# Token mix of an fp32 mixer block: eight chunks of 512 output tokens and a separate stage for the last 128

## Chip, cores, metric

The kernel runs on one core of a Trainium2 chip. The metric is device time in microseconds (us) of one execution of the program; lower is better.

## What is computed

Three layers follow each other on x of shape [4, 4224, 192] (B batches, S tokens, D channels). Weights come as float64 and are unpacked on the chip.

```python
# 1. causal convolution over 7 tokens, softmaxed taps, one set of taps per head
out[b, s, h, g] = sum_k w[h, k] * x_pad[b, s + k, h, g]
# 2. token mix over all 4224 tokens, then a channel mix
theta = x @ w_theta                      # 192 x 192
zr, zi = x * cos(theta), x * sin(theta)
y = einsum('ts,bsd->btd', w_tok_r, zr) + einsum('ts,bsd->btd', w_tok_i, zi)   # two 4224 x 4224 weights
u = x + y;  x = u + relu(u @ w_ch)
# 3. low-rank token mix (rank 32) and a feed-forward layer 192 -> 768 -> 192
u = x + ((x.T @ U) @ V).T;  x = u + relu(u @ w_ch1) @ w_ch2
```

## The kernel before

**Data.** y is kept in one SBUF tile `yt` of 128 partitions by 6 by 4224: the 4 x 192 = 768 (batch, channel) columns are six blocks of 128 partitions, the tokens lie along the free axis. The source tokens are 33 blocks s of 128. For each block, two "units" (one per half of the batches) run a prep: convolution on VectorE (14 instructions), a split into a high and a low part, theta on TensorE (10 matmuls), range reduction on VectorE, sine and cosine on ScalarE, products on VectorE, and again a split. The result is `z` of block s: 128 source tokens by 4 (real high, imaginary high, real low, imaginary low) by 768.

**Token mix.** A group (g, j, r) makes one PSUM tile `acc` of 128 (batch, channel) columns by one chunk of output tokens. In `products` (line 709 is its matmul) a 128 x 128 block of z is stationary and the weights of the chunk move: for each source block and for real and imaginary weights the three products z_high w_high, z_high w_low, z_low w_high, all in fp32r. With two source blocks (kb = 2) that is 12 matmuls. `evict` (line 717 on VectorE, 719 on ScalarE for the first source block) adds the group to `yt`. PSUM gives `acc` four buffers.

**Steps.** `mix_steps` lists the steps. In the steady part a stage takes two source blocks through nine chunks (`WIDTHS`: 480, six of 464, two of 480), so nine steps g; the last two source blocks use eleven chunks of 384 (`LATE`), interleaved with the layers that follow. A step has six slots j. In each slot the group comes first, then the weight jobs of `SPLITS[j]`, then the prep functions that `plan` holds for that slot. All engines take their instructions strictly in this written order.

**Weights.** A step needs two pieces (q = 0 real, q = 1 imaginary), each up to 960 raw float64 words per partition, loaded on SP's queue into one of two `wraw` buffers. `split_w` does four parts: 0, two ScalarE instructions (lines 250 and 255); 1, sign and join on VectorE (264 and 269); 2, the high part by a ScalarE cast (652); 3, the low part by a VectorE subtraction (655), behind which the next load is issued. Both pieces of a step share one tile `wt[g]` of two buffers. For step g + 1, `SPLITS` spreads the parts over the slots of step g:

```python
SPLITS = [
    [(1, 0, 2)], [(1, 0, 3), (1, 1, 0)], [(1, 1, 1)], [(1, 1, 2)], [(1, 1, 3), (2, 0, 0)], [(2, 0, 1)],
]
```

Each entry is (steps ahead, q, part). So the low part of the second piece is made in slot 4, and slot 5 lies between it and the step that reads it.

**Around it.** `OPENING` is a hand-written order of the start: the first three steps, the first four units, their weights. `unit_slots` places the 20 stages of every later unit in slots; four units are spread over a stage, 12 slots apart. `ENTRY` and `TURN` are written orders for the last two source blocks, the channel mix, the low-rank mix and the start of the feed-forward layer, whose matmuls (lines 1158 to 1162 and 1195 to 1201) have 384 moving columns.

Of the kernel before, what the change touches and what calls it, by code (L numbers as in the profile page):

```python
# [10 lines left out]
F32 = mybir.dt.float32  # L11
F32R = mybir.dt.float32r
I32 = mybir.dt.int32
# [20 lines left out]
WIDTHS = [480] + [464] * 6 + [480] * 2  # L34
# [5 lines left out]
def mix_steps():  # L40
# [15 lines left out]
EARLY = 5  # L56
STEPS, STARTS = mix_steps()

# [30 lines left out]
WSTEP = 480  # L89

LSTEP = 448
# [3 lines left out]
SPLITS = [  # L95
    [(1, 0, 2)], [(1, 0, 3), (1, 1, 0)], [(1, 1, 1)], [(1, 1, 2)], [(1, 1, 3), (2, 0, 0)], [(2, 0, 1)],
]
PREP_AT = -4
UNIT = 12

STAGES = 20


def unit_slots():

    def steady(n0):
        return [n0 + n for n in range(STAGES)]

    n0 = SLOTS * OPENED
    units = [(2, 0, [n0 + n // 2 for n in range(TAPS)] + steady(n0 + 4)[: STAGES - TAPS])]  # L110
    units += [(2, 1, [n0 + 8 + n // 2 for n in range(TAPS)] + steady(n0 + 12)[: STAGES - TAPS])]
    n0 = SLOTS * STARTS[1]
    units += [(3 + u // 2, u % 2, steady(n0 - 8 + (21 * u) // 2)) for u in range(4)]
    for k in range(2, len(STARTS) - 1):
        n0 = SLOTS * STARTS[k] + PREP_AT
        units += [(2 * k + 1 + u // 2, u % 2, steady(n0 + UNIT * u)) for u in range(4)]
    return units

# [106 lines left out]
def mix_kernel(ctx, tc, xT, wcv, wth, wtok, wch, uu, vv, w1, w2, outT):  # L225
# [68 lines left out]
    wp = pool("wp", bufs=2, stack=left)  # L294
    wrp = pool("wraw", bufs=2, stack=raw_st)
# [5 lines left out]
    ps_th = pool("ps_th", bufs=2, space=PSUM, stack=prep_st)  # L301
# [4 lines left out]
    with tc.manual_schedule():  # L306
# [12 lines left out]
        wc_raw = taps(3300)  # L319
# [32 lines left out]

        def load_w(h):
            if h >= len(pieces):
                return
            kb, n, src = pieces[h]
            if h in (2, 3):
                t = spare(h - 2, 2336, 4 * WIDTHS[1]).bitcast(I32).rearrange("p (n w) -> p n w", w=2)
            else:
                t = wrp.tile([P, 2 * WMAX, 2], I32, name="wraw", tag="wraw")  # L360
# [1069 lines left out]
```

## Time and profile before

| | us |
|---|---|
| time, median of 3 runs | 2961.15 |
| lowest and highest run | 2960.17 and 2961.39 |
| span of the profiled execution, first to last instruction | 2958.9 |
| that execution: TensorE busy (matmuls) | 2947.7 |
| VectorE busy | 2494.5 |
| ScalarE busy | 1547.0 |
| GpSimd busy | 308.4 |

The profile is of one execution; its span leaves out what lies around the first and last instruction, 2.25 us against the median of the runs. PE is TensorE, PEld its weight loads, DVE is VectorE, ACT ScalarE, POOL GpSimd, SP the engine whose queue issues the loads. A matmul's "mean" is its own time from start to modelled end, and neighbours overlap in the pipeline: what a stream of them costs is read from a stretch's length divided by the count in it.

### The profile page before, as it was taken

The numbers are of one execution on the slowest core, as the hardware profiler recorded it, in microseconds if no ns is written. First come the engines' busy times: TensorE is split into PE (matmuls) and PEld (weight loads), VectorE is DVE, ScalarE is ACT, GpSimd is POOL, SyncE is SP. The second block draws the span as 40 slices with busy tenths as digits, with TensorE's granted clock in tenths as the row PEclk, the third lists the DMA queues.
The fourth block names the chain that finished last, engine by engine and source line by source line (L and its number), as shares of the span: only waits on it lengthen the run. The fifth ranks groups of instructions, "written<-read, shape, count | busy, mean of one in ns | idle before, by whom it ended". The sixth has DMA issues, their size and how long they took to land.

```text
span 2958.9 us, 39058 instructions
## 1 busy us (share of the span) xinstructions
PE 2947.7 (100%) x14994; PEld 2689.5 (91%) x14994; DVE 2494.5 (84%) x4132; ACT 1547.0 (52%) x2230; POOL 308.4 (10%) x263
## 2 busy tenths in 40 slices
PE   9999999999999999999999999999999999999999
PEld 8888888888888889898989898888889999999999
DVE  8899989888888988898989898989899887555555
ACT  7655545455555555554555554545456555444443
POOL 2110000010000000000000010100002111001000
PEclk9999999999999999999999999999999999999999
DMA  4443443443434434434434334344343221101110
GB/s 137 134 132 123 128 132 125 128 132 122 136 124 127 135 125 127 133 122 131 129 124 132 128 124 135 124 128 135 122 129 107 74 65 50 37 31 43 35 38 33
DMA packets 119003, 323.51 MB, mean 109 GB/s; under 512 B 6688, under 2 KB 40480, under 8 KB 118688
## 3 DMA queue, kind: packets, MB, share of 16 engines
q1 hardware_dynamic: 118416, 320.81, 33.7%
q8 instruction: 118, 1.93, 0.3%
q14 instruction: 69, 0.57, 0.1%
q10 hardware_dynamic: 400, 0.21, 0.0%
HBM read 308.01 MB, written 12.98 MB: 108 GB/s over the span
## 4 chain that ended last, share of the span: by engine, by line
PE 95%; DVE 3%; issue 0%; ACT 0%; DMA 0%; POOL 0%; DVEq 0%; POOLq 0%; ACTq 0%
PE acc L709 74%; PE ob L1196 2%; PE acc L1158 2%; PE acc L1162 2%; PE oa L1198 2%; PE ob L1195 2%; PE oa L1201 2%; PE oa L1200 2%; PE acc L1159 2%; PE acc L1160 2%; PE acc L1161 1%; PE pacc L916 1%; PE th L541 1%; PE th L542 1%; PE tr L901 1%; PE th L544 1%
## 5 line engine op out<-in xcount | busy, mean ns | idle before, releaser
L709 PE MATMUL acc<-w,z 128*128 128x464 f32 (+2 forms) x10836 | 2286.7, 371 | 1.8 <-POOL z L603 0.8
L709 PEld LDWEIGHTS acc<-w,z 128*128 128x128 f32 x10836 | 2015.6, 188 | 241.4 <-DVE yt L717 1.5
L717 DVE TENSOR_TENSOR yt<-acc,yt 128x464 f32<-128x464 f32 (+2 forms) x876 | 551.9, 636 | 211.8 <-PE acc L709 208.4
L652 ACT CAST w<-wraw 128x928 fp32r<-128x928 f32 (+3 forms) x281 | 294.6, 1049 | 625.4 <-DVE wraw L269 625.4
L264 DVE TENSOR_SCALAR wraw<-wraw 128x928 uint16<-128x928 uint16 (+3 forms) x305 | 369.5, 1212 | 12.3 <-ACT wraw L255 6.2
L250 ACT ACTIVATE wraw<-wraw,consts 128x928 int32<-128x928 uint16 (+3 forms) x305 | 349.1, 1144 | 23.9 <-DMA wraw<-in_wtok 16.7
L655 DVE TENSOR_TENSOR w<-wraw,w 128x928 fp32r<-128x928 f32 (+2 forms) x272 | 356.5, 1310 | 0.0
L269 DVE SCALAR_TENSOR_TENSOR wraw<-wraw 128x928 int32<-128x928 int32 (+3 forms) x305 | 342.0, 1121 | 9.8
L255 ACT ACTIVATE wraw<-wraw 128x928 f32<-128x928 f32 (+4 forms) x289 | 304.4, 1053 | 4.1 <-DMA wraw<-in_wtok 1.9
L603 POOL TENSOR_TENSOR z<-tz,z 128x384 fp32r<-128x384 f32 x121 | 125.2, 1034 | 1706.3 <-ACT z L600 1706.3
L478 DVE SCALAR_TENSOR_TENSOR xa<-xr,tap,xa 128x256 f32<-128x256 f32 x744 | 286.7, 428 | 0.0
L1170 DVE SCALAR_TENSOR_TENSOR hid<-acc,hid 128x384 fp32r<-128x384 f32 x264 | 146.8, 557 | 148.9 <-ACT hid L1167 148.0
L1167 ACT ACTIVATE hid<-acc 128x384 fp32r<-128x384 f32 x264 | 129.7, 492 | 250.1 <-PE acc L1162 232.8
L600 ACT CAST z<-tz 128x384 fp32r<-128x384 f32 x129 | 66.3, 514 | 289.0 <-DVE tz L589 288.9
L609 POOL TENSOR_TENSOR yt<-yt,xa 128x384 f32<-128x384 f32 x64 | 70.2, 1096 | 248.6 <-DVE xa L478 195.4
L1196 PE MATMUL ob<-hid,cl 128*128 128x384 f32 x264 | 89.2, 338 | 0.1
L1158 PE MATMUL acc<-fq,w 128*128 128x384 f32 x264 | 89.1, 338 | 0.0
L1162 PE MATMUL acc<-fq,w 128*128 128x384 f32 x264 | 89.0, 337 | 0.0
L1198 PE MATMUL oa<-hid,cl 128*128 128x384 f32 x264 | 88.7, 336 | 0.0
L1201 PE MATMUL oa<-hid,cl 128*128 128x384 f32 x264 | 88.7, 336 | 0.0
L1200 PE MATMUL oa<-hid,cl 128*128 128x384 f32 x264 | 88.7, 336 | 0.0
L1195 PE MATMUL ob<-hid,cl 128*128 128x384 f32 x264 | 88.6, 336 | 0.0
(244 smaller groups left out, 2685.9 us busy)
## 6 DMA issues: line engine op xcount, KB each, us to landing
wraw<-in_wtok SPq DMA_DIRECT2D x184, 928.0 KB, 4.7
wraw<-in_wtok SPq DMA_DIRECT2D x92, 960.0 KB, 4.8
wraw<-in_wtok SPq DMA_DIRECT2D x22, 768.0 KB, 4.4
xr<-in_xT SPq DMA_DIRECT2D x63, 201.0 KB, 2.7
outT<-ot SPq DMA_DIRECT2D x20, 576.0 KB, 3.1
vzw<-in_vv SPq DMA_DIRECT2D x10, 384.0 KB, 4.1
wraw<-in_w SPq DMA_DIRECT2D x3, 768.0 KB, 4.3
yt<-in_wtok SPq DMA_DIRECT2D x2, 928.0 KB, 8.6
```

Of the source, the lines that this page charges most:

```text
L250: nc.scalar.activation(words(raw, 0), words(raw, 1, U16), AF.Identity, scale=2.0**-13, bias=consts[:, 3:4])
L255: nc.scalar.activation(w, w, AF.Copy, scale=2.0**-112)
L264: nc.vector.tensor_scalar(out=words(raw, 1, U16), in0=words(raw, 3, U16), scalar1=0x8000, scalar2=None, op0=ALU.bitwise_and)
L269: nc.vector.scalar_tensor_tensor(out=words(raw, 1), in0=words(raw, 1), scalar=3, in1=words(raw, 0), op0=ALU.logical_shift_left, op1=ALU.bi ...
L478: nc.vector.scalar_tensor_tensor(out=xa, in0=src, scalar=w, in1=xa, op0=ALU.mult, op1=ALU.add)
L652: nc.scalar.copy(hi, src)
L655: eng.tensor_tensor(out=weight_part(g, q, 1), in0=src, in1=f(hi), op=ALU.subtract)
L709: mm(ps, a, b[:, i + r, :], start=n == 0, stop=n == last)
L717: nc.vector.tensor_tensor(out=dst, in0=ps, in1=dst, op=ALU.add)
L1158: mm(ps, w[0], q[:, b, :], start=True, stop=False)
L1162: mm(ps, w[3], q[:, 4 + b, :], start=False, stop=True)
L1196: mm(ob, c2[:, m, 2, :], h[:, 1, :], start=False, stop=last)
```

## The change

`WIDTHS` becomes eight chunks of 512. They cover 4096 tokens; the last 128 (`TAIL`) of 31 of the 33 source blocks go through a new function `tail`, once in each stage (15 times): there a 128 x 128 block of weights is stationary, z moves with 384 columns, and the sums come out with the tokens on the partitions. They are kept so in the last columns of `yt` and transposed once at the end (`tail_turn`). Each piece of weights gets a tile of its own (`wt[g, q]`), with four buffers of half the size, and a spare tile shifts their addresses. Two temporaries of the prep move: `ta` shares the buffer of `xq`, `tb` goes to PSUM, and theta's PSUM tile loses its second buffer. So sine and cosine now share one buffer and come one after the other. The weight jobs are listed by step (`split_plan`), with three more job slots in a step that has a tail; the units' slots are packed differently. In the opening, `EARLY` is 4, so its third step has one chunk instead of two. The two source blocks at the end keep their eleven chunks of 384.

```diff
-WIDTHS = [480] + [464] * 6 + [480] * 2
+WIDTHS = [512] * 8
+TAIL = sum(WIDTHS)
...
-EARLY = 5
+EARLY = 4
 STEPS, STARTS = mix_steps()
+TAILS = {STARTS[1] + EARLY - 1: (0, 3)} | {n + 3: (2 * k + 3, 2) for k, n in enumerate(STARTS[2:-1])}
...
-WSTEP = 480
-
-LSTEP = 448
+WSTEP = 512
+HALF = 4 * WSTEP
+SHIFT = 16
...
+def split_plan():
+
+    def following(g):
+        return ("t", g + 1) if g + 1 in TAILS else 2 * (g + 2)
+
+    plan = {}
+    for g in range(OPENED, STARTS[-1]):
+        a, b, c = 2 * (g + 1), 2 * (g + 1) + 1, following(g)
+        if g in TAILS:
+            t = ("t", g)
+            jobs = [[(t, 2)], [(t, 3), (a, 0)], [(a, 1)], [(a, 2)], [(a, 3), (b, 0)], [(b, 1)]]
+            jobs += [[(b, 2)], [(b, 3), (c, 0)], [(c, 1)]]
+        elif g == STARTS[-1] - 1:
+            jobs = [[(a, 0)], [(a, 1), (b, 0)], [(a, 2), (b, 1)], [(a, 3), (b, 2)], [(b, 3)], [(c, 0), (c, 1)]]
+        else:
+            jobs = [[(a, 2)], [(a, 3), (b, 0)], [(b, 1)], [(b, 2)], [(b, 3), (c, 0)], [(c, 1)]]
...
-PREP_AT = -4
+SPLITS = split_plan()
+PREP_AT = -8
 UNIT = 12
-STAGES = 20
+STEADY = list(range(20))
+QUICK = [*range(TAPS), 7, 8, 8, 9, 10, 11, 11, 11, 12, 13, 14, 15, 16]
...
-    units += [(3 + u // 2, u % 2, steady(n0 - 8 + (21 * u) // 2)) for u in range(4)]
+    units += [(3 + u // 2, u % 2, slots(n0 - 9 + 9 * u, QUICK)) for u in range(4)]
...
-    wp = pool("wp", bufs=2, stack=left)
-    wrp = pool("wraw", bufs=2, stack=raw_st)
+    wp = pool("wp", bufs=4, stack=left)
+    wp.tile([P, 32], F32, name="align", tag="align", bufs=1)
+    raws = {"pool": pool("wraw", bufs=2, stack=raw_st), "n": 2 * WMAX}
...
-    ps_th = pool("ps_th", bufs=2, space=PSUM, stack=prep_st)
+    ps_th = pool("ps_th", space=PSUM, stack=prep_st)
+    ps_x = pool("ps_x", space=PSUM, stack=prep_st)
...
-            stages += [(("sincos",),), (("rot", 0), ("z_hi", 0)), (("z_lo", 0, eng),)]
+            stages += [(("sincos", 0), ("sincos", 2)), (("rot", 0), ("z_hi", 0)), (("sincos", 1), ("z_lo", 0, eng))]
...
+        def tail_products(g, r):
+            s0, kb = TAILS[g]
+            key = "t", g
+            ps = sums[key, r] = ps_mm.tile([P, WMAX], F32, name="acc", tag="acc")[:, :COLS]
+            n, last = 0, 6 * kb - 1
+            for u in range(2 * kb):
+                z, q = zt[s0 + u // 2], u % 2
+                zh, zl = (z[:, m, r * COLS : (r + 1) * COLS] for m in (q, 2 + q))
+                high, low = (tail_part(key, m)[:, u, :] for m in range(2))
+                for a, b in ((high, zh), (high, zl), (low, zh)):
+                    mm(ps, a, b, start=n == 0, stop=n == last)
+                    n += 1
...
+        def tail(g):
+            tail_products(g, 0)
+            split_jobs(g, SLOTS)
+            tail_products(g, 1)
+            tail_evict(g, 0)
+            split_jobs(g, SLOTS + 1)
+            tail_evict(g, 1)
+            split_jobs(g, SLOTS + 2)
+            del wt["t", g]
 
         def mix(steps):
             for g in steps:
                 for j in range(SLOTS):
                     for r in range(len(STEPS[g][2])):
                         group(g, j, r)
-                    for d, q, part in SPLITS[j]:
-                        split_w(g + d, q, part)
+                    split_jobs(g, j)
+                    if g == max(TAILS) + 1 and j < 2:
+                        tail_turn(j)
                     for fn in plan.get(g * SLOTS + j, ()):
                         fn()
-                del wt[g]
+                for q in range(2):
+                    del wt[g, q]
+                if g in TAILS:
+                    tail(g)
```

## Rows read from the trace of the kernel before

**Rows 1.** The page: span, and each engine's busy time, share of span and instructions.

```profile
span 2958.9 us, 39058 instructions
PE 2947.7 (100%) x14994; PEld 2689.5 (91%) x14994; DVE 2494.5 (84%) x4132; ACT 1547.0 (52%) x2230; POOL 308.4 (10%) x263
```

**Rows 2.** The page: the chain that ended last, by engine.

```profile
PE 95%; DVE 3%; issue 0%; ACT 0%; DMA 0%; POOL 0%; DVEq 0%; POOLq 0%; ACTq 0%
```

**Rows 3.** Waits of TensorE in the token mix: us in total, times, longest.

```profile
PE acc L709 <- POOL z L603: 0.8, 1, 0.8
PE acc L709 <- DVE yt L717: 0.7, 1, 0.7
```

**Rows 4.** Groups of TensorE by line and shape: count, busy us, mean ns, idle before.

```profile
L709 PE MATMUL acc<-w,z 128*128 128x464 f32 x6696 | 1411.4, 371 | 0.8 <-DVE yt L717 0.7
L709 PE MATMUL acc<-w,z 128*128 128x480 f32 x3348 | 731.7, 379 | 1.0 <-POOL z L603 0.8 <-ACT z L600 0.2
L709 PE MATMUL acc<-w,z 128*128 128x384 f32 x792 | 149.2, 339 | 0.0
```

**Rows 5.** Stretches: length; busy us (count) of PE, PEld, DVE, ACT, POOL; granted clock; DMA.

```profile
415.69:430.74 15.04, 15.04 (x73) 13.51 (x72) 14.97 (x28) 7.88 (x13) 2.05 (x2) 1.00 0.45 140
510.31:525.91 15.60, 15.60 (x73) 13.52 (x72) 13.38 (x21) 8.71 (x11) 2.04 (x2) 1.00 0.38 125
383.77:525.91 142.14, 142.14 (x689) 126.64 (x688) 126.76 (x205) 73.67 (x94) 13.05 (x12) 1.00 0.40 128
2560.00:2950.00 390.00, 390.00 (x2252) 390.00 (x2251) 227.10 (x425) 174.28 (x343) 33.29 (x18) 1.00 0.10 35
```

**Rows 6.** Groups of VectorE by shape within the stage 383.77 to 525.91 us.

```profile
L717 DVE TENSOR_TENSOR yt<-acc,yt 128x464 f32<-128x464 f32 x36 | 22.7, 637 | 8.0 <-PE acc L709 7.9
L717 DVE TENSOR_TENSOR yt<-acc,yt 128x480 f32<-128x480 f32 x18 | 11.8, 654 | 6.5 <-PE acc L709 6.5
L655 DVE TENSOR_TENSOR w<-wraw,w 128x960 fp32r<-128x960 f32 x6 | 8.2, 1363 | 0.0
L264 DVE TENSOR_SCALAR wraw<-wraw 128x960 uint16<-128x960 uint16 x6 | 7.5, 1256 | 0.0
L269 DVE SCALAR_TENSOR_TENSOR wraw<-wraw 128x960 int32<-128x960 int32 x6 | 7.0, 1160 | 0.2
```

**Rows 7.** The same stage, ScalarE: the cast to the high part.

```profile
L652 ACT CAST w<-wraw 128x960 fp32r<-128x960 f32 x6 | 6.4, 1072 | 9.9 <-DVE wraw L269 9.9
```

**Rows 8.** Timeline 1000 to 1006 us: eviction, sign, join, cast to high.

```profile
1001.09 0.64 DVE L717 TENSOR_TENSOR yt<-acc,yt 128x464 f32<-128x464 f32 x1
1001.65 1.22 DVE L264 TENSOR_SCALAR wraw<-wraw 128x928 uint16<-128x928 uint16 x1
...
1002.90 1.13 DVE L269 SCALAR_TENSOR_TENSOR wraw<-wraw 128x928 int32<-128x928 int32 x1
...
1004.12 1.03 ACT L652 CAST w<-wraw 128x928 fp32r<-128x928 f32 x1 [3.20 <-DVE wraw L269]
```

**Rows 9.** Timeline of VectorE, 404 to 432 us: evictions early and late, a low part.

```profile
408.38 0.64 DVE L717 TENSOR_TENSOR yt<-acc,yt 128x464 f32<-128x464 f32 x1 [0.84 <-PE acc L709]
...
424.46 0.63 DVE L717 TENSOR_TENSOR yt<-acc,yt 128x464 f32<-128x464 f32 x1
...
428.49 1.18 DVE L717 TENSOR_TENSOR yt<-acc,yt 128x464 f32<-128x464 f32 x2
429.58 1.12 DVE L655 TENSOR_TENSOR w<-wraw,w 128x928 fp32r<-128x928 f32 x1
```

**Rows 10.** The same columns: the opening, and the end of the second stage.

```profile
23.00:45.00 22.00, 21.14 (x101) 18.28 (x102) 21.23 (x41) 19.74 (x39) 4.60 (x4) 1.00 0.24 92
170.00:210.00 40.00, 40.00 (x197) 36.04 (x196) 39.40 (x69) 21.44 (x28) 3.21 (x3) 1.00 0.38 126
210.00:241.60 31.60, 30.83 (x148) 26.68 (x147) 31.37 (x53) 16.67 (x23) 4.08 (x4) 1.00 0.38 129
```

**Rows 11.** The page: loads of weight pieces, KB each, median us from issue to landing.

```profile
wraw<-in_wtok SPq DMA_DIRECT2D x92, 960.0 KB, 4.8
```

More of the change, by code (lines that the diff above doesn't have):

```diff
@@ new lines @@
+    dg0.0 dg1.0 dg1.5 SL dg0.2 u0.pc0 dg1.1 dg1.6 dg0.1 dg0.5 dg1.4@act dg0.6@act dg0.4@act dg1.3@act dg0.3 dg1.2@act
+    u0.pc1 u0.pc2 u0.pc3 u0.pc4 T.low u0.pc5 T.scale@dve T.sign W0.low u0.pc6 T.join T.t3 W1.scale T.t1 u1.pc0 W1.low
+    u0.xhi2 T.t2@pool u1.pc1 W0.scale@dve T.t4@pool W0.sign W0.join u1.pc2 u0.xhi0@dve u0.xlo0 u0.xlo2 u0.xhi1 u1.pc3
+    W1.sign u0.xcp u0.xlo1 W2.scale@dve W2.low W1.join u0.theta u1.pc4 W3.scale u0.turn0 W2.sign u0.turn1 W3.low
+    W2.join u1.pc5 u1.pc6 u0.red0 u0.red1 u0.red2 u1.xhi2@dve u1.xhi0 W0.hi W1.hi u1.xhi1@dve u0.abs u1.xlo2 A.pc0
@@ new lines @@
+    u1.xlo0 u0.cos W0.lo@pool A.pc1 u1.xlo1 u0.rot0 W1.lo@pool A.pc2 u1.xcp A.pc3 A.pc4 A.pc5 A.pc6 u0.sin W3.sign
+    u0.zhi0 A.xhi1 A.xhi2 A.xlo1 A.xlo2 A.xhi0 u0.zlo0@pool A.xcp u0.rot1 u1.theta u1.turn0 u0.zhi1 g0_0.0a u1.turn1
+    u0.zlo1@pool W2.hi W3.join A.xlo0 u1.red0 g0_1.0a g0_2.0a g0_0.0 g0_1.0 u1.red1 u1.red2 W3.hi u1.abs eg0_0.0 W2.lo
+    W3.lo u1.sin g0_2.0 eg0_1.0@dve eg0_2.0@dve u1.cos u1.rot0 A.xadd g1_0.0a u1.rot1 A.theta A.turn0 g1_0.1a g1_0.0
+    W4.low g1_0.1 u1.zhi0 g1_1.0a eg1_0.1 A.turn1@dve g1_1.1a B.convb0 u1.zhi1 B.conva0 eg1_0.0 u1.zlo0 g1_1.0 A.red0
@@ L85 @@
+    eg1_5.0 A.zlo0 eg1_5.1 B.xhi0 B.xlo0 A.rot1 g2_1.0a g2_1.0 eg2_0.0 g2_2.0a W6.scale@dve g2_2.0 W6.low A.zhi1
+    eg2_1.0 B.theta W7.scale W7.low W6.sign W6.join W6.hi eg2_2.0 g2_3.0a A.zlo1 B.turn0 B.xadd W7.sign g2_3.0 B.turn1
+    W6.lo g2_4.0a W7.join B.red0 B.red1 W7.hi B.red2 g2_4.0 eg2_3.0 B.abs eg2_4.0@dve B.cos B.sin B.rot0 W8.scale@dve
+    W8.low B.zhi0 W8.sign g2_5.0a g2_5.0 W7.lo@pool W8.join B.zlo0 B.rot1 eg2_5.0 u1.xadd@dve B.zhi1 u0.xadd@dve
+    B.zlo1
 """.split()
@@ L351, in mix_kernel @@
         pieces += [(2, COLS, flat(w2, 0, 2 * COLS)), (1, COLS, flat(w2, 4 * P * COLS, COLS))]
+        wu = wtok.rearrange("(u p n w) -> p u n w", p=P, n=S, w=2)
+        tails = {
+            ("t", g): (2 * kb, P, wu[:, 2 * s0 : 2 * (s0 + kb), TAIL:, :]) for g, (s0, kb) in TAILS.items()
+        }
+        stream = [0, 1]
+        for h in range(4, len(pieces)):
+            stream.append(h)
+            if ("t", h // 2) in tails and h % 2:
+                stream.append(("t", h // 2))
+        follows = dict(zip(stream, stream[2:]))
         def load_w(h):
-            if h >= len(pieces):
+            if h not in tails and h >= len(pieces):
                 return
-            kb, n, src = pieces[h]
+            kb, n, src = tails[h] if h in tails else pieces[h]
             if h in (2, 3):
-                t = spare(h - 2, 2336, 4 * WIDTHS[1]).bitcast(I32).rearrange("p (n w) -> p n w", w=2)
+                t = spare(h - 2, 2176, 4 * WMAX).bitcast(I32).rearrange("p (n w) -> p n w", w=2)
             else:
-                t = wrp.tile([P, 2 * WMAX, 2], I32, name="wraw", tag="wraw")
+                t = raws["pool"].tile([P, raws["n"], 2], I32, name="wraw", tag="wraw")
             raw[h] = t[:, : kb * n, :]
@@ L1090, in mix_kernel @@
         group(STARTS[-1], 0, 0)
-        for d, q, part in SPLITS[0]:
-            split_w(STARTS[-1] + d, q, part)
+        split_w(2 * STARTS[-1] + 2, 2)
         for fn in plan.get(LAST, ()):
@@ L1276, in open_hid @@
             fo = late_fo["hid"] = pool("fin", stack=fin)
[L1277 removed]
+            fo.tile([P, 16], F32, name="room", tag="room")
         h0 = 2 * n_chunks
```

164 lines of the change are left out of this document (90 added, 74 removed).

## Prediction

> **What bounds the kernel now.** I read the page first. TensorE is busy for 2947.7 of 2958.9 us, and VectorE comes next with 2494.5 [rows 1]; the chain that ended last is 95% TensorE [rows 2]. A busy TensorE says little by itself, so I looked at its waits: in the whole token mix it waited less than 2 us, the longest wait 0.8 us [rows 3]. So what its stream of matmuls costs, and any new wait put into it, go straight into the time.
>
> What does a matmul in the stream cost? The means of the groups are its latency (371 and 379 ns), not that [rows 4]. I took stretches with nothing but one width [rows 5]; each holds six slots of 12 matmuls, and the count of 73 includes the one that still runs at the edge. A step of 464 columns takes 15.04 us / 72 = 208.9 ns, a step of 480 takes 15.60 / 72 = 216.7 ns, and the feed-forward layer with 384 columns 390 / 2252 = 173.2 ns. The granted clock is 1.00 in all of them, the 2.4 GHz level, at which one column takes 0.417 ns. Per column the three cost 0.4502, 0.4514 and 0.4510 ns. That is the central reading: the price is proportional to the columns, about 0.451 ns each, in a stretch where VectorE is 99% busy and in one where it is 58% busy. There is hardly a fixed price per matmul that wider chunks could save.
>
> VectorE is the second engine to watch. In a steady stage it is busy for 126.8 of 142.14 us [rows 5], and evictions start late: a slot of the step at 415.69 lasts 15.04 / 6 = 2.51 us, so slots end at 423.22, 425.72 and 428.23. The evictions for the first two start at 424.46 and 428.49, which is 1.24 and 2.77 us after TensorE's last matmul of the slot was issued and followed by the next; one that finds VectorE idle starts 0.2 us after (408.38, where the slot, three before 415.69, ended at 408.17) [rows 9]. Four PSUM buffers hide this lag today.
>
> **The change part by part.**
>
> *Fewer, wider matmuls.* Removed: the 6696 + 3348 = 10044 matmuls of the first 31 source blocks [rows 4]; the 792 of 384 columns stay. They cost 6696 x 0.2089 + 3348 x 0.2167 = 1398.8 + 725.5 = 2124.3 us. Added: 31 blocks x 2 pieces x 3 products x 6 slots x 8 chunks = 8928 matmuls of 512 columns, and in the tails 31 x 2 x 3 x 2 = 372 of 384 columns, 64.4 us at 173.2 ns. No row has 512 columns. By the per-column price of the 480 step, the nearest, it is 512 x 0.4514 = 231.1 ns; 8928 x 0.2311 = 2063.3. The sum is 2127.7, which is **+3.4 us**: the columns are the same (9 chunks and 8 chunks plus tail both make 4224). Bounds for 512: the 464 step's 0.4502 gives 230.5 ns, which is 2 us less than before; a line through 464 and 480 (7.8 ns for 16 columns) gives 232.3 ns, +14 us. I take the proportional value.
>
> The row of the 384 stretch shows 13.2 ns more than 384 / 2.4, and the 480 step 16.7 more than 200. The Trainium skill (TensorE: Matmul & The Clock Gate, section "Wait — 56ns, not 53.3ns?") has a fixed 2.5 ns per matmul beyond its columns at the full clock, measured on bf16. By that rule 744 fewer matmuls would save 1.9 us and a 512-column one would take 215.8 ns; this trace's fp32r streams are slower and grow with the width, so the sum doesn't use it.
>
> *The weights of the step behind a tail.* This is a new wait, and TensorE has no slack to pay it from. In an ordinary step the order stays as it was: the second piece's low part in slot 4. In a step with a tail all jobs shift: sign and join of the second piece in slot 5, its high part between the two halves of the tail, its low part behind the first tail eviction. Call S the moment when TensorE is through with slot 5. On its side lie 24 tail matmuls x 173.2 = 4.16 us, six matmuls of the next step's first piece, and one with the second piece's high part, 7 x 231.1 = 1.62: it needs the low part at S + 5.78. On the other side stands a chain that can't start before slot 5's eviction, since VectorE takes its orders in turn. From eviction to sign 0.56 us with 464 columns (1001.09 to 1001.65), 0.60 with 512 [rows 8]. Sign, join, cast and low part at 960 elements are 1.256, 1.160, 1.072 and 1.363 us [rows 6, 7]; at 1024 (x 1.067) 1.34, 1.24, 1.14 and 1.45. The handover from join to ScalarE takes 0.09 (1002.90 + 1.13 to 1004.12) [rows 8]; I use it three times, with the one to TensorE, and 0.03 between sign and join. Sum: 0.60 + 1.34 + 0.03 + 1.24 + 1.14 + 1.45 + 0.27 = 6.07 us. The tail's first eviction fits beside the cast. The eviction starts 0.2 us after S at best and 2.8 at worst [rows 9]. Slot 3 of that step carries only an eviction and one tap, slot 4 an eviction, a low part, a rotation and a tap, some half a us over its time, so I take 0.6. The low part is then ready at S + 6.67, **0.9 us late**. Bounds: 0.2 and the fastest low part shown (1.12 x 1024 / 928 = 1.24 us, rows 9) give 0.3 late; 2.8 gives 3.1. With kb = 3 the first tail has 36 matmuls, 6.2 us, and covers the chain. The other 14 tails stall: 14 x 0.9 = **+12.6 us** (4 to 43).
>
> *Opening.* Five chunks of the first block become four: 36 x 2336 columns become 36 x 2048, so 4.7 us of TensorE's work move from the opening to later. In the 22 us from 23 to 45 VectorE is busy for 21.2 and ScalarE for 19.7 [rows 10]: if they set the pace there, TensorE idles for what was moved. But two weight pieces shrink from 928 to 512 elements too, which frees the same engines. Between 0 and 4.7, nearer to 0: **+0.5**. The first pieces grow by 32 columns, 0.03 us per instruction, inside this.
>
> *Second stage.* There VectorE is already full: 39.4 of 40 us, then 31.4 of 31.6 with TensorE short by 0.8 [rows 10]. Its units come 9 slots apart instead of 10.5; a slot grows from about 2.55 to 2.77, so 24.9 us instead of 26.8 per unit. The total of work is the same. Between -0.8 (the wait goes) and +4: **+1**.
>
> *At nothing.* Evictions: 54 of 0.64 to 0.65 us in a stage become 48 of about 0.69 and two of 384, VectorE's sum stays within 1 us [rows 6]; it is off the path while the lag stays under three slots. `tb` in PSUM, sine after cosine, one buffer for theta: a unit's theta tile lives from stage 10 to 18 and units are 12 slots apart, so nothing meets; without that cover each unit would wait about a slot. Halves of weight buffers free earlier, never later. The two loads behind the pool switch at the end land within some 5 to 10 us [rows 11], with more than two slots of slack behind them. Tail loads are smaller pieces on a queue that has room (DMA share 0.40, rows 5). Six transposes come once, under 1 us.
>
> **Sum.** 3.4 + 12.6 + 0.5 + 1.0 = 17.5. On the profiled execution's 2958.9 this makes a span of 2976.4; with the 2.25 us that lie between span and median, 2961.15 + 17.5 = **2979 us**.
>
> **Rivals.**
>
> 1. *The tail's stall is hidden* (the chain is shorter, or the lag is near 0.2). Then only streaming and the opening are left, 2961 + 0 to 5 = 2961 to 2966. For it: the estimate is 0.3 us at its lower bound, close to none. Against it: each piece of the chain has a row, and VectorE is 89% busy.
>
> 2. *A fixed price per matmul after all: faster.* The 464 and 480 chunks follow each other at a stride of 480 x 4 = 1920 bytes, so their start addresses shift against each other; the feed-forward operands (1536 bytes) and the new chunks (2048 bytes) repeat at multiples of 512. If the surplus is a fixed 13.2 ns, as in the 384 stretch, and the rest of 464 and 480 comes from addresses, 512 columns cost 213.3 + 13.2 = 226.5 ns: 8928 x 0.2265 + 64.4 = 2086.6, 37.7 less; with stalls of 12.6 and the 1.5 the time is 2938, without 2925. It decides from 229.1 ns down if the stalls come (14.1 us to save), from 230.5 if they don't. Against it: three widths on one line through zero would be a coincidence. The skill's rule above is of this kind, a fixed price, though a smaller one.
>
> 3. *VectorE falls behind everywhere.* If the denser units, the serial sine and cosine, and accesses to `tb` in PSUM add more than the 15 us that a stage leaves free, each stage grows by the excess; two us more in each of 14 stages besides the tail stall gives 2979 + 28 = 3007. For it: the second stage is at 99%. Against it: the steady work per stage is unchanged.
>
> **Chances.** The forecast 0.46, rival 1 0.24, rival 2 0.18, rival 3 0.12. A measurement of this kernel tells a change from none at about 0.2%, 5.9 us. Faster (under 2955.2): rival 2 mostly, and a little of 1, 0.21. Within: most of rival 1, the upper end of 2, and the forecast at its lowest stall, 0.22. Slower (over 2967.1): 0.57. The likeliest case's own range is 2966 to 2996 (stalls of 0.3 to 2 us); the range for 8 in 10 goes from 2943, inside rival 2, to 2999.
>
> **What would show it.** Stretches of a 512 step without theta: 72 matmuls in 16.64 us if the price is per column, 16.3 if it is fixed. In TensorE's waits, the 512-column matmul waiting for the VectorE subtraction that makes the low part, 14 times, about 0.9 us each, all just behind a tail; a stage of 142.3 us plus this wait. VectorE busy for some 127 us per stage. The prediction is wrong if a 512 step comes under 16.5 us, if that wait doesn't appear, or if TensorE waits for z, theta or PSUM buffers instead.

## Result and profile after

The kernel with eight chunks of 512 takes **2986.14 us** (median of 4 runs, 2985.36 to 2986.61) against 2960.93 before: ratio 1.0085, 95% interval 1.0070 to 1.0099, 25.2 us slower. The forecast was 2979 with a range of 2943 to 2999. The number is near by luck: one term was 39 us too high and four others together 43 us too low, as the sections below show. One run of the kernel e7_tail_cast (experiment 2), the one with the profile, had a granted clock of 0.75 throughout and took 3625 us; that kernel's figures leave it out.

The page of the kernel after, span and engines, and its shares of the chain that ended last:

```profile
span 2984.6 us, 37445 instructions
PE 2934.1 (98%) x14256; PEld 2550.8 (85%) x14256; DVE 2497.6 (84%) x4023; ACT 1521.3 (51%) x2185; POOL 358.1 (12%) x263
...
PE 81%; DVE 9%; ACT 1%; issue 1%; DMA 1%; POOL 0%; SPq 0%; ACTq 0%; DVEq 0%; POOLq 0%
```

TensorE is busy for 13.6 us less than before while the span is 25.7 us longer [rows 1]. So the matmuls became cheaper and something else took more than they gave back. The chain says the same: TensorE sets 81% of it in place of 95%, VectorE 9% in place of 3% [rows 2]. TensorE's waits name the places (us in total, times, longest):

```profile
PE acc L765 <- DVE w L705: 10.9, 15, 0.8
PE th L588 <- DVE xq L570: 7.9, 6, 2.2
PE acc L765 <- ACT w L700: 4.8, 12, 0.4
PE th L587 <- ACT xq L548: 4.2, 1, 4.2
PE th L587 <- ACT xa L542: 4.2, 1, 4.2
PE th L587 <- DVE yt L635: 2.2, 1, 2.2
PE acc L765 <- POOL w L705: 2.2, 1, 2.2
PE acc L765 <- DVE yt L773: 2.1, 2, 1.3
```

Line 765 is the product, 700 and 705 make the high and low part of the weights, 587 and 588 are theta, 548 and 570 make the high and low part of its operand, 542 is ScalarE's copy of the convolution out of PSUM, 635 the rotation, which is the last to read theta's PSUM tile, and 773 the eviction. Before, the two longest rows in the token mix were 0.8 and 0.7 us [rows 3]. The first and third row come 15 and 12 times, once in most stages; the others come once or a few times, all ahead of 271 us.

To see where each microsecond lies I took the first matmul of each stage as its start. Lengths in us; the last six lines belong to the experiments below (the reordering e7 has none, as said there):

| kernel | start to end of the opening | second stage | 14 steady stages | from there to TensorE's last matmul |
|---|---|---|---|---|
| before | 128.8 | 112.9 | 1990.0 | 722.4 |
| after | 143.4 | 127.5 | 1983.3 | 725.5 |
| e1_tail_early | 145.1 | 127.3 | 1970.4 | 724.7 |
| e2_x_late | 143.0 | 128.2 | 1983.2 | 725.4 |
| e3_theta_two | 136.8 | 127.5 | 1983.3 | 724.4 |
| e8_x_all | 144.9 | 122.5 | 1983.2 | 724.4 |
| e10_all | 138.7 | 119.7 | 1960.6 | 724.4 |
| e11_theta_later | 137.0 | 115.7 | 1960.6 | 724.4 |

The opening lost 14.7 us and the second stage 14.6; the steady stages, where I had put nearly all of the loss, gained 6.6; the last part lost 3.1. Together 25.7, the difference of the spans.

**Steady stages.** Stretches of one stage: a step of 512 columns without theta, the step with the tail, the step behind it, the whole stage (length; busy us and count of PE, PEld, DVE, ACT, POOL; granted clock; DMA):

```profile
855.46:871.78 16.32, 16.32 (x74) 13.52 (x72) 16.25 (x29) 8.39 (x10) 1.03 (x1) 1.00 0.39 130
889.41:909.89 20.48, 20.48 (x98) 17.68 (x96) 19.08 (x35) 9.35 (x14) 3.97 (x3) 1.00 0.47 156
909.89:929.29 19.40, 18.24 (x83) 14.70 (x83) 15.20 (x21) 11.04 (x11) 0.00 (x0) 1.00 0.36 118
837.83:979.59 141.76, 140.60 (x641) 117.27 (x640) 127.07 (x198) 71.98 (x92) 15.79 (x12) 1.00 0.39 129
```

The first stretch answers to the 464 and 480 steps of [rows 5]: 16.32 / 72 = **226.7 ns** for 512 columns, 0.4427 ns per column in place of 0.451. The tail's 24 matmuls take 20.48 - 16.32 = 4.16 us, as forecast. The step behind the tail has a theta in it, and other steps with one take 17.63 (855.46 - 837.83); this one takes 19.40, so the stall costs **1.77 us**, not 0.9. Twelve of the 14 such steps take 19.37 to 19.56, two 18.86; together they stall for some 24 us.

The stall by its instructions, in the timeline (start, length, engine, instruction):

```profile
905.73 4.33 PE L858 MATMUL acc<-z,wtail 128*128 128x384 f32 x24
...
906.53 0.68 DVE L773 TENSOR_TENSOR yt<-acc,yt 128x512 f32<-128x512 f32 x1
906.57 1.02 POOL L649 TENSOR_TENSOR z<-tz,z 128x384 fp32r<-128x384 f32 x1 [3.43 <-ACT z L646]
...
907.13 1.67 DVE L290 TENSOR_SCALAR wraw<-wraw 128x1024 uint16<-128x1024 uint16 x1
907.55 1.96 POOL L655 TENSOR_TENSOR yt<-yt,xa 128x384 f32<-128x384 f32 x1
908.83 1.77 DVE L295 SCALAR_TENSOR_TENSOR wraw<-wraw 128x1024 int32<-128x1024 int32 x1
...
910.69 1.11 ACT L700 CAST w<-wraw 128x1024 fp32r<-128x1024 f32 x1 [3.35 <-DVE wraw L295]
...
911.83 1.22 DVE L705 TENSOR_TENSOR w<-wraw,w 128x1024 fp32r<-128x1024 f32 x1 [0.77 <-ACT w L700]
...
913.11 1.21 PE L765 MATMUL acc<-w,z 128*128 128x512 f32 x4 [0.76 <-DVE w L705]
```

The chain runs in the order that the prediction wrote down: eviction, sign, join, cast, low part, TensorE. TensorE leaves slot 5 at 905.73, and the low part is done at 911.83 + 1.22 = 913.05, 7.32 us later, where 6.67 were forecast. The eviction starts 0.80 behind the slot in place of 0.60; sign and join take 1.67 and 1.77 in place of 1.34 and 1.24, together 0.86 more; the low part takes 0.23 less than scaled. The two that grew run beside POOL. When the sign starts at 907.13, POOL is in the low part of z (line 649, 906.57 to 907.59); when the join starts at 908.83, POOL is in its addition (line 655, 907.55 to 909.51). That addition takes 1.96 here and 1.03 in a reordered kernel where VectorE does other work (886.55 there, run e11_theta_later below). Each of the two ends as if it had stood still until POOL was done: the sign would end at 907.59 + 1.34 = 908.93 and ended at 908.80, the join at 909.51 + 1.24 = 910.75 and ended at 910.60. Where VectorE starts no later than POOL, POOL is the one that takes longer: in e11_theta_later a low part and POOL's line 652 both start at 884.49, the first takes its usual 1.22 us, the second 2.10 in place of 1.02. The Trainium skill (SBUF — State Buffer, section "SBUF: two separate sides") has VectorE and GpSimd share a pair of ports that the instruction which starts first holds to its end while the other stands still; of VectorE's instructions it names those with two SBUF inputs, as the join has, and those in a two-port mode. The trace agrees for the join within 0.15 us; the sign has one input and is held in the same way, and whether it runs in such a mode no run shows.

**Opening and second stage.** Three stretches (same columns), the first the one shown in [rows 10] for the kernel before:

```profile
23.00:45.00 22.00, 16.78 (x68) 14.11 (x69) 16.14 (x32) 11.96 (x25) 4.97 (x5) 0.84 0.18 58
224.00:239.00 15.00, 11.35 (x49) 8.65 (x47) 10.39 (x14) 6.21 (x8) 1.99 (x2) 0.97 0.42 154
239.00:248.40 9.40, 6.60 (x19) 5.48 (x20) 5.42 (x8) 5.62 (x9) 0.00 (x0) 0.50 0.00 1
```

From 23 to 45 us VectorE is busy for 16.1 us where it was 21.2, ScalarE for 12.0 where it was 19.7: no engine is short of time, they all wait for each other. And the granted clock falls: 0.84 here, and 0.50 (the 1.2 GHz level) through 239 to 248.4, where a wait of 4.2 us ends at 239.8. Before, it stood at 1.00 in these stretches [rows 10]. A wait in this kernel is paid once as idle time and, when it is long, again as slow matmuls.

What TensorE waited for at 239.8 can be followed in the timeline:

```profile
231.51 0.38 SPq L358 DMA_DIRECT2D xr<-in_xT  x1
231.99 2.95 SPq L404 DMA_DIRECT2D wraw<-in_wtok  x2
...
237.27 1.19 ACT L276 ACTIVATE wraw<-wraw,consts 128x1024 int32<-128x1024 uint16 x1 [5.89 <-DMA wraw<-in_wtok]
238.37 1.08 ACT L281 ACTIVATE wraw<-wraw 128x1024 f32<-128x1024 f32 x1
239.36 0.91 ACT L548 CAST xq<-xa 128x256 fp32r<-128x256 f32 x3
...
239.80 0.64 PE L587 MATMUL th<-t,xq 128*128 128x320 f32 x1 [4.20 <-ACT xq L548]
```

ScalarE stands 5.89 us before the first job of a weight piece, because the load (line 404) was issued only at 231.99. Ahead of it on SP's queue stands a load of x (line 358) for unit (5, 0), which has to wait until the convolution of unit (4, 1) has left the one `xr` buffer. Theta's operand is cast behind the weight jobs on ScalarE, and theta and all products behind it wait.

### The profile page after: what moved, and what is told of

It reads as the page before. It is cut to its first block, busy times and chain, and to the rows that moved or that the text cites. A ratio compares the mean times of both kernels' runs of the same rounds, so it can differ in the third digit from the quotient of the medians.

```text
span 2984.6 us, 37445 instructions
## 1 busy us (share of the span) xinstructions
PE 2934.1 (98%) x14256; PEld 2550.8 (85%) x14256; DVE 2497.6 (84%) x4023; ACT 1521.3 (51%) x2185; POOL 358.1 (12%) x263
## 4 chain that ended last, share of the span: by engine, by line
PE 81%; DVE 9%; ACT 1%; issue 1%; DMA 1%; POOL 0%; SPq 0%; ACTq 0%; DVEq 0%; POOLq 0%
PE acc L765 60%; DVE wraw L290 2%; DVE wraw L295 2%; PE ob L1297 2%; PE acc L1259 2%; PE acc L1263 2%; PE oa L1299 2%; PE ob L1296 2%; PE oa L1302 2%; PE oa L1301 2%; PE acc L1260 2%; PE acc L1261 1%; PE acc L1262 1%; DVE yt L773 1%; DVE w L705 1%
## 5 line engine op out<-in xcount | busy, mean ns | idle before, releaser
L765 PE MATMUL acc<-w,z 128*128 128x512 f32 (+1 forms) x9720 | 2205.9, 387 | 20.0 <-DVE w L705 10.9
L765 PEld LDWEIGHTS acc<-w,z 128*128 128x128 f32 x9720 | 1809.7, 188 | 378.1 <-DVE w L705 15.9
L773 DVE TENSOR_TENSOR yt<-acc,yt 128x512 f32<-128x512 f32 (+1 forms) x786 | 527.7, 673 | 200.0 <-PE acc L765 195.5
L700 ACT CAST w<-wraw 128x1024 fp32r<-128x1024 f32 (+2 forms) x251 | 279.9, 1115 | 647.4 <-DVE wraw L295 632.0
L290 DVE TENSOR_SCALAR wraw<-wraw 128x1024 uint16<-128x1024 uint16 (+2 forms) x290 | 388.2, 1339 | 29.2 <-ACT wraw L281 24.4
L295 DVE SCALAR_TENSOR_TENSOR wraw<-wraw 128x1024 int32<-128x1024 int32 (+2 forms) x290 | 365.8, 1261 | 9.3
L276 ACT ACTIVATE wraw<-wraw,consts 128x1024 int32<-128x1024 uint16 (+2 forms) x290 | 340.6, 1174 | 57.4 <-DMA wraw<-in_wtok 46.8
L705 DVE TENSOR_TENSOR w<-wraw,w 128x1024 fp32r<-128x1024 f32 (+2 forms) x242 | 293.8, 1214 | 11.6 <-ACT w L700 11.6
L281 ACT ACTIVATE wraw<-wraw 128x1024 f32<-128x1024 f32 (+3 forms) x274 | 300.8, 1098 | 3.4 <-DMA wraw<-in_wtok 2.5
L655 POOL TENSOR_TENSOR yt<-yt,xa 128x384 f32<-128x384 f32 x64 | 120.3, 1880 | 76.0 <-DVE xa L524 25.4
```

Source lines behind the costliest of these rows:

```text
L276: nc.scalar.activation(words(raw, 0), words(raw, 1, U16), AF.Identity, scale=2.0**-13, bias=consts[:, 3:4])
L281: nc.scalar.activation(w, w, AF.Copy, scale=2.0**-112)
L290: nc.vector.tensor_scalar(out=words(raw, 1, U16), in0=words(raw, 3, U16), scalar1=0x8000, scalar2=None, op0=ALU.bitwise_and)
L295: nc.vector.scalar_tensor_tensor(out=words(raw, 1), in0=words(raw, 1), scalar=3, in1=words(raw, 0), op0=ALU.logical_shift_left, op1=ALU.bi ...
L700: nc.scalar.copy(hi, src)
L705: eng.tensor_tensor(out=lo, in0=src, in1=f(hi), op=ALU.subtract)
```

## Experiments

Nine kernels ran, each an edit of the kernel after.

**1. The tail step's jobs, two things earlier** (e1_tail_early).

```diff
-jobs = [[(t, 2)], [(t, 3), (a, 0)], [(a, 1)], [(a, 2)], [(a, 3), (b, 0)], [(b, 1)]]
-jobs += [[(b, 2)], [(b, 3), (c, 0)], [(c, 1)]]
+jobs = [[(t, 2)], [(t, 3), (a, 0)], [(a, 1)], [(a, 2), (b, 0)], [(a, 3), (b, 1)], [(b, 2)]]
+jobs += [[(b, 3), (c, 0)], [], [(c, 1)]]
```

> In a step with a tail, the second piece of weights is unpacked one slot earlier (its parts 0 and 1 in slots 3 and 4, its cast in slot 5, its low part in the first slot of the tail). In the changed kernel the step behind each tail lasts 19.40 us, and 17.63 us (16.32 plus theta) would be a step without a wait. Theory A, the wait is the chain sign, join, cast, low part that starts too late: the step behind a tail falls to about 17.63 us at all 14 tails, VectorE's low part leaves the list of TensorE's waits, and the time falls by 14 x 1.77 = 25 us, to about 2961 us. Rival B, VectorE is simply full around a tail, so that an earlier job only delays another one: the 1.77 us come back as waits for evictions or for theta in the same or the next step, and the time stays within 5 us of 2986.

Measured 2973.0 us (2971.41 to 2974.2), ratio to before 1.0040 (1.0026 to 1.0055), 13.1 us less than after. The step behind the tail takes 18.51: half of the stall is gone. Where the other half lies:

```profile
765.20 0.28 DVE L635 TENSOR_TENSOR tz<-th,ta 128x128 f32<-128x128 f32 x1
...
765.51 0.51 ACT L646 CAST z<-tz 128x384 fp32r<-128x384 f32 x1 [2.86 <-DVE tz L635]
765.93 1.15 ACT L700 CAST w<-wraw 128x1024 fp32r<-128x1024 f32 x1
...
767.09 1.02 POOL L655 TENSOR_TENSOR yt<-yt,xa 128x384 f32<-128x384 f32 x1
767.11 2.08 DVE L705 TENSOR_TENSOR w<-wraw,w 128x1024 fp32r<-128x1024 f32 x1 [0.37 <-ACT w L700]
...
769.25 2.11 PE L765 MATMUL acc<-w,z 128*128 128x512 f32 x8 [0.54 <-DVE w L705]
```

The cast of the weights now stands on ScalarE behind the cast of z (line 646), which waits 2.86 us for a rotation on VectorE. And the low part takes 2.08 us in place of 1.22, beside POOL's addition, which started 0.02 us ahead of it.

**2. The same with the cast ahead of that of z, and the low part right behind slot 5** (e7_tail_cast).

```diff
+jobs = [[(t, 2)], [(t, 3), (a, 0)], [(a, 1)], [(a, 2), (b, 0)], [(a, 3), (b, 1), (b, 2)], [(b, 3)]]
+jobs += [[(c, 0)], [], [(c, 1)]]
```

> Theory (order of the splitting): the 1.77 us that PE loses in each step behind a tail are there because ACT casts the second half's high part behind z_hi, which waits for the rotation, and DVE gets to the low part only beside POOL's z_lo. With the cast in slot 4, ahead of z_hi, and the low part right behind the eviction of slot 5, both are done before the tail's products end: the step behind a tail takes 17.63 us as every step with a theta does, 14 x 1.77 = 24.8 us come off 2986.1, and the time is 2961 (2957 to 2966), the time of the kernel before. Rival (DVE and ACT have no room): whatever the order, a tail step holds more work for DVE than its 20.5 us let through; the step behind the tail stays near the 18.51 us of the first reordering, and the time near 2973.

Measured 2958.07 us (median of nine runs, 2956.17 to 2961.46), 28.1 less than after; ratio to before 0.9993 (0.9983 to 1.0002), no difference. The kernels e10 and e11 hold the same edit, and in the second of them the tail step, the step behind it and the stage read:

```profile
864.24:884.72 20.48, 20.48 (x98) 17.68 (x96) 19.09 (x36) 9.88 (x14) 1.25 (x2) 1.00 0.46 153
884.72:902.38 17.66, 17.66 (x83) 14.78 (x83) 14.09 (x20) 10.62 (x13) 2.85 (x2) 1.00 0.41 133
812.66:952.65 139.99, 139.99 (x642) 117.32 (x640) 125.95 (x198) 72.06 (x92) 15.98 (x12) 1.00 0.40 130
```

TensorE is busy for the whole of each stretch and the step behind the tail is down to 17.66. The stall was a matter of the written order, not of VectorE's capacity: the same jobs fit without a wait. In the steady stages of e10 and e11 this takes off 1983.3 - 1960.6 = 22.7 us; why the time of this kernel alone fell by some 5 us more isn't shown.

**3. Loads of x later in the second stage** (e2_x_late and e8_x_all, each with its own line for `lead`).

```diff
-at(max(SLOTS * OPENED, slots[0] - 5), load)
+lead = 2 if i in (2, 3, 4) else 5                                          # e2_x_late
+lead = 2 if (i, p) in ((3, 0), (3, 1), (4, 0), (4, 1), (5, 0)) else 5     # e8_x_all
+at(max(SLOTS * OPENED, slots[0] - lead), load)
```

> In the second stage and ahead of it (source blocks 2 to 4), the load of x for a unit is issued 2 slots ahead of the unit's first tap instead of 5. Theory A: with units 9 slots apart, a load issued 5 slots ahead waits on SP's queue until the unit before has read the one buffer of x, and the weight loads stand behind it; the weights come late, TensorE waits, its granted clock halves. Then the wait of 5.9 us of ScalarE for the weights near 231 us goes, the half-clock stretch at 238 to 248 us goes, and the second stage falls from 127.5 us to about 116 to 120, the time by 8 to 12 us, to about 2974 to 2978 us. Rival B: the second stage is long because VectorE has no room for units 9 slots apart; then the stage stays within 3 us of 127.5 us with the waits moved to the low part of x (matmuls of theta), and the time is 2983 to 2987 us.

Measured 2985.51 us (2985.39 to 2986.52), the second stage at 128.2: nothing gained. The load that stood in the way was that of unit (5, 0), the first unit of the next stage, which this edit (units of blocks 2 to 4) left where it was; ScalarE still waited 5.5 us.

> Theory (SP's queue): in the second stage the weight load stands on SP behind the x load of unit (5,0), which waits for the convolution of unit (4,1). With that load 2 slots ahead of its unit in place of 5 it comes behind the weight load; ACT's wait of 5.9 us at 231, PE's gap of 4.36 us and the 10.24 us at half clock behind it go: 4.36 + 5.1 = 9.5 us, second stage 118 in place of 127.5, time 2976.6 (2973 to 2980). Rival (the load is only the last of several that are late): DVE's and ACT's work in this stage is itself late, theta finds its operands no earlier than a few us before, second stage over 124, time over 2982.

Measured 2981.61 us (2980.6 to 2981.81), the second stage at 122.5. ScalarE's wait for the load there is down from 5.9 to 0.3 us; of the 9.5 us expected 5.0 came. In the kernel after and in e8, ScalarE's waits from 229 to 245 us:

```profile
ACT wraw L276 <- DMA wraw<-in_wtok: 5.9, 1, 5.9
ACT w L700 <- DVE wraw L295: 4.1, 2, 2.3
```

```profile
ACT w L700 <- DVE wraw L295: 6.2, 2, 3.9
...
ACT wraw L276 <- DMA wraw<-in_wtok: 0.3, 1, 0.3
```

ScalarE now waits for VectorE, and theta for VectorE's low part of its operand, 2.9 us, with a shorter stretch at the lower clock behind it. The queue was one cause; VectorE, late by a few us at theta's fixed slot, is the next.

**4. A second PSUM buffer for theta in the opening** (e3_theta_two), and A's theta and first turn where the kernel before has them (lines shortened).

```diff
-th = ps_th.tile([P, 2, 512], ...)
+th = (ps_o if i < 2 and p else ps_th).tile([P, 2, 512], ...)   # ps_o is closed after open_mix
-u1.rot0 A.xadd g1_0.0a u1.rot1 A.theta A.turn0 g1_0.1a
+g0_2.0a A.theta g0_0.0 ... g0_2.0 A.turn0 eg0_1.0@dve ... u1.rot1 g1_0.1a
```

> In the opening alone, theta gets its second PSUM buffer back (the bank that tb takes later is still free there), and theta of the third unit goes back to its place in the order of the kernel before. Theory A: the opening lost 14.7 us because TensorE, in its written order, stood at theta of the second unit until the first unit's last product had freed the single buffer (4.4 us), and the clock then fell to half three times. Then the stretch up to the second stage falls from 143.4 us to about 131 to 134 us (128.8 in the kernel before), with no half-clock stretch near 26 us, and the time to about 2974 to 2977 us. Rival B: the wider first weight pieces and the single chunk in the third step set the opening; then it falls by the 4.4 us of that one wait at most, to 2981 us or more.

Measured 2978.55 us (2978.27 to 2979.75), ratio 1.0060 (1.0044 to 1.0077); the opening ends at 136.8 in place of 143.4 (the kernels here that don't change the opening end it between 143.0 and 145.1). TensorE's longest waits from 15 to 130 us:

```profile
PE acc L767 <- POOL w L707: 2.2, 1, 2.2
PE th L590 <- DVE xq L572: 1.9, 2, 1.0
```

The two waits of theta for lines 542 and 635 (4.2 and 2.2 us in the kernel after) are gone. So the single buffer that I had costed at nothing, with the later place of A's theta that came with it, takes 6.7 of the 14.7 us lost there; the two edits weren't run apart.

**5. The price of a width** (e4_480_even, e9_widths).

```diff
-mm(ps, a, b[:, i + r, :], ...)
+mm(ps[:, :m], a, b[:, i + r, :m], ...)      # m < 512 for all but a group's first product
```

In e4 m is 480 from the fourth step on; in e9 it is one of fourteen widths, one for each steady stage, in two of its steps. The left-out columns get part of their sums only.

> For the first 31 source blocks every product of a group but the first leaves out the last 32 of its 512 columns (from the fourth step on), so 11 of 12 matmuls have 480 columns; their start addresses still repeat at multiples of 2048 bytes. Theory F, a matmul costs its columns at 2.4 GHz and a fixed 13.3 ns, and the chunks of the kernel before paid more because their starts shifted against each other: a step without theta takes 6 x (226.7 + 11 x 213.3) ns = 15.44 us. Rival P, the price is per column as in the kernel before (216.7 ns for 480) and full chunks of 512 are an exception: 6 x (226.7 + 11 x 216.7) ns = 15.66 us. Time is about 50 us under the changed kernel's either way, as columns are left out.

Measured 15.72 us for a step without theta:

```profile
699.78:715.50 15.72, 15.72 (x74) 13.52 (x73) 15.65 (x28) 7.62 (x10) 1.02 (x1) 1.00 0.40 134
```

Six products are full, so one of 480 takes (15.72 - 6 x 0.2267) / 66 = 217.6 ns, although the start addresses here repeat at multiples of 2048 bytes. That is the 216.7 of before, within 1 ns, not 213.3. The address explanation of the second rival is refuted.

> In steps 1 and 5 of each of the fourteen steady stages every product but the first of a group moves fewer columns than 512, one width for each stage (508, 504, 496, 488, 472, 456, 448, 432, 416, 400, 352, 320, 256, 192), so the rest of the output columns get a part of their sum only. Time of one product, by three theories. Per column with 512 as the only exception (columns/2.4 x 13/12): 508 229.3 ns, 504 227.5, 496 223.9, 488 220.3, 448 202.2, 416 187.8, 320 144.4, 256 115.6, 192 86.7. Fixed price of 13.3 ns for multiples of 128 only: as above, but 256 at 120.0. Fixed price for multiples of 64: also 448 at 200.0, 320 at 146.7, 192 at 93.3. The whole time only follows the sum and decides nothing.

Steps at m = 508, 496, 488, 448 and 400, in this order:

```profile
286.87:303.34 16.47, 16.47 (x73) 13.53 (x72) 16.40 (x30) 8.37 (x10) 1.02 (x1) 1.00 0.38 129
570.80:586.68 15.88, 15.88 (x73) 13.52 (x72) 15.81 (x28) 7.81 (x10) 1.02 (x1) 1.00 0.40 133
711.64:727.93 16.29, 16.29 (x74) 13.61 (x73) 16.22 (x29) 8.24 (x10) 1.02 (x1) 1.00 0.39 130
1132.18:1147.13 14.95, 14.95 (x73) 13.52 (x72) 14.88 (x27) 7.01 (x9) 1.02 (x1) 1.00 0.43 141
1548.34:1561.66 13.32, 13.32 (x73) 13.05 (x72) 13.25 (x24) 5.26 (x7) 0.37 (x1) 1.00 0.46 158
```

With the same division, and columns / 2.4 taken off:

| columns | 512 | 508 | 496 | 488 | 480 (e4) | 448 | 400 | 384 (tail) |
|---|---|---|---|---|---|---|---|---|
| ns per product | 226.7 | 228.9 | 220.0 | 226.2 | 217.6 | 205.9 | 181.2 | 173.3 |
| over columns / 2.4 | 13.3 | 17.3 | 13.3 | 22.9 | 17.6 | 19.2 | 14.5 | 13.3 |

The two steps of each width agree. The widths not shown, down to 320, lie between 13.8 ns over (320) and 17.7 (504 and 456). At 256 and 192 VectorE, busy for 9.35 of 9.38 and 9.34 of 9.37 us, sets the step, so the division says nothing there; at 256 the intervals between products, without one long one in each step, average 119.7 ns, 13.0 over. None of the three theories holds: 496 is no multiple of 64 and pays the least, 448 is one and pays 19.2, and 488 columns cost more than 496. What the runs show is a floor of about 13.3 ns over columns / 2.4, which 512, 496, 384, 256 and nearly 320 reach and other widths miss by up to 10 ns. Why they miss it stays open.

**6. All together** (e10_all): experiment 2, e8_x_all and e3_theta_two, and the low part of weight half 7 moved from POOL to VectorE.

```diff
-W7.join B.red0 B.red1 W7.hi B.red2 g2_4.0 eg2_3.0 B.abs ... g2_5.0 W7.lo@pool W8.join
+W7.join B.red0 W7.hi B.red1 B.red2 g2_4.0 eg2_3.0 W7.lo B.abs ... g2_5.0 W8.join
```

> All that was found taken together: the splitting behind a tail in the order of the run e7_tail_cast (24.8 us), the x loads of the second stage later (9.5), a second PSUM buffer for theta in the opening with A's theta where it was before (7.6 as measured alone), and the low part of weight half 7 on DVE, earlier, in place of POOL (1 to 3). If these add up: 2986.1 - 44 = 2942 (2935 to 2950), ratio to the kernel before 0.9936, so a kernel in 512-column chunks that beats both. Rival (they are one slack shared: what one gives the next wait takes): over 2955.

Measured 2950.72 us (2949.85 to 2954.03), ratio to before 0.9968 (0.9955 to 0.9980): faster than both, but 9 us short of the sum. The opening got worse than in e3 (138.7 against 136.8). The last edit had moved a wait, not removed it. From the timeline, and a stretch right behind it:

```profile
82.59 1.45 PE L768 MATMUL acc<-w,z 128*128 128x512 f32 x5 [1.45 <-DVE w L707]
```

```profile
83.80:91.20 7.40, 5.23 (x18) 4.30 (x18) 6.39 (x9) 2.48 (x4) 2.45 (x1) 0.56 0.49 146
```

VectorE, which took the low part over from POOL, is late with the next ones at 80 us, theta behind it waits 2.2 us, and the clock falls there instead of at 66 us.

**7. Without that edit, and theta one slot later in the second stage** (e11_theta_later).

```diff
-QUICK = [*range(TAPS), 7, 8, 8,  9, 10, 11, 11, 11, 12, 13, 14, 15, 16]
+LATER = [*range(TAPS), 7, 8, 8, 10, 11, 12, 12, 12, 12, 13, 14, 15, 16]   # units of the second stage
```

> The run e10_all without the change to weight half 7 (in its trace that only moved PE's gap from 63 us to 80 us and put another stretch at half clock behind it), and with the theta products and what follows them one slot later for the four units of the second stage. Theory (what is left in the second stage is theta standing in its slot before DVE has its low part: 2.2, 1.7, 2.2 us and less): the four waits go, one slot is 2.72 us; second stage 119.7 - 6 = 113 to 115; opening as in e3_theta_two, 137; time 2950.7 - 6 - 2 = 2943 (2939 to 2947). Rival (DVE falls behind by as much again, the wait moves to the accumulation that needs its evictions or to the rotation at the end of the stage): second stage 118 or more, time 2947 to 2955.

Measured **2944.11 us** (2943.12 to 2945.48), ratio to before 0.9942 (0.9928 to 0.9956), inside the range of the theory. The second stage is down to 115.7, just over the 113 to 115 expected. TensorE's waits from 136 to 262 us, and the stretch that ends with this stage:

```profile
PE acc L769 <- DVE yt L777: 2.3, 3, 1.3
PE acc L769 <- DVE w L708: 0.9, 1, 0.9
PE th L591 <- DVE xq L573: 0.2, 1, 0.2
```

```profile
210.00:252.70 42.70, 40.08 (x178) 31.66 (x177) 42.11 (x69) 22.22 (x30) 6.10 (x5) 1.00 0.38 128
```

Theta's waits for VectorE went from 6.1 us in e10 to 0.2 (two edits differ between the two kernels; these waits are what the later slot acts on), the clock is at 1.00, and VectorE is busy for 42.1 of 42.7 us: now this stage is short of VectorE itself, as [rows 10] showed for the kernel before.

## Why the prediction was right or wrong

The time lay inside the range, 7 us over the forecast, by luck: errors in both directions cancelled. By its steps:

- **Fewer, wider matmuls: wrong in sign.** The term was +3.4 us at 231.1 ns. At 226.7 ns it is 8928 x 0.2267 + 64.4 - 2124.3 = -35.9. The step that failed is the reading of three widths as one line through zero. 384, 464 and 480 do lie on it, but by coincidence: the widths tried in e9 lie on no line at all. The price of the second rival (226.5) is the one that happened; its reason, start addresses, is refuted by e4. A stretch under 16.5 us was named as what would prove this step wrong, and it came at 16.32. The Trainium skill (TensorE: Matmul & The Clock Gate, section "Wait — 56ns, not 53.3ns?") was nearer in kind, a fixed price per matmul, for the widths at the floor; its 2.5 ns is 13.3 here, in fp32r.
- **The weights behind a tail: mechanism right, size half.** The wait is there in the place and in the order given, some 24 us in place of 12.6, inside the bounds of 4 to 43. What was missing is 0.86 us for sign and join, which stood behind POOL's instructions, and 0.2 for the eviction, less 0.23 for a faster low part; the sum took VectorE's lengths from rows and had no term for POOL. Experiment 2 takes the wait out, 22.7 us in the steady stages of e10 and e11.
- **Opening: wrong.** +14.7 in place of +0.5, and outside the bounds of 0 to 4.7. I had looked only at whether the engines have time, and they do. Theta's one PSUM buffer, costed at nothing because "nothing meets" in the steady stages, meets in the opening, where the units follow each other closely: 6.7 us (e3, together with the place of A's theta). The other 8.0 stay; in e3 TensorE still waits for 6.0 us there, 2.2 of them for a low part on POOL; that the third step now has half as many products to cover the preparations is argued, not shown, and a third step with two chunks wasn't tried.
- **Second stage: wrong.** +14.6 in place of +1. The denser units fit VectorE's sum, but not the order: a load behind another on SP's queue (5.0 us, e8), and theta in a slot that comes before VectorE has its operand (the same stage went from 119.7 in e10 to 115.7 in e11). The last of the three signs of being wrong that the prediction named came true here too: TensorE waits for PSUM buffers, twice for an eviction, 2.1 us, and in the opening for theta's.
- **At nothing.** In the steady stages the evictions kept their cover, and so did the loads at the end. The last part grew by 3.1 us, 2.0 in the later runs, for which the sum had no term. In its first 18 us TensorE has two waits for VectorE that the kernel before doesn't have (0.7 at line 990, 0.4 at line 966), and 1.8 of the 3.1 are lost there; the rest wasn't traced.
- **Clock.** The sum had no term for it. From 16 to 144 us and from 144 to 271 the granted clock is 0.96 on average, where before it was 1.00. An estimate from this, 0.04 x 128 = 5 us, is about the most that slow matmuls can have cost in each of the two. The waits of 4.2 us had stretches at 1.2 GHz beside them; of those near 2.2 us the one that ended at 72.8 did, the one that ended at 175.0 did not.

So -39 us on one term stood against +43 on four others: some 12 for the stall, 14 each for the opening and the second stage, 3 for the last part (some 4 more if one takes the cheaper products of the 3 blocks there out of these, 39 x 3 / 31). The forecast is near because they cancel. Of the rivals, the first (no stall) was wrong, the second right in price and wrong in its reason and its time, the third wrong: VectorE stayed at 127 us per stage.

## What to carry to other kernels

Measure the price of the very width that a change moves to: neighbours on a line don't vouch for the next one, and 488 columns can cost more than 496. When buffers are merged or units set closer, check the densest stretch of the program, not the steady one, and follow each queue in its order, that of POOL too: a stage with idle engines can still be slow because of what stands ahead of what. A change that makes the main stream cheaper may come out slower only by such waits; here taking them out turned +25 us into -17.

## What the runs showed of the hardware that was not expected

The price of an fp32r product over columns / 2.4 goes from 13.3 ns (512, 496, 384) to 22.9 (488) and isn't monotone in the width. A VectorE instruction of 1024 elements that started while a POOL instruction ran ended up to 0.86 us later (2.08 against 1.22 for the low part), about as if it had stood still until POOL's end; where VectorE started no later than POOL, VectorE kept its length and POOL's doubled (2.10 against 1.02). The sign, with a single input, was held as well as the join. TensorE's clock stood at 0.50 for the 9.4 us from 239, where a wait of 4.2 us ended, and in e11 at 1.00 through the second stage, where the longest wait was 1.3 us.
